# Six early loads and one copy change their places in a hand-ordered attention and feed-forward kernel

## The chip, the cores and the metric

The kernel runs on one core of one Trainium2 chip. The metric is device time in microseconds (us) of one execution. The kernel before was timed three times: median 570.61 us, 570.03 to 570.77. TensorE is written PE, VectorE DVE, ScalarE ACT, GpSimd POOL and SyncE SP; SP issues nearly every transfer between memory and the core.

## The reference, cut to what matters

An attention with a matrix state (4 batches, 8 heads, 768 steps, 40 elements a head) makes x, and a feed-forward part with a rational activation follows:

```python
for t in range(S):
    m_new = np.maximum(f_gate[:, :, t] + m, i_gate[:, :, t])
    f_stab = np.exp(f_gate[:, :, t] + m - m_new)
    i_stab = np.exp(i_gate[:, :, t] - m_new)
    m = m_new
    C = f_stab * C + i_stab * outer(v[t], k[t])      # 40 x 40 a head
    n = f_stab * n + i_stab * k[t]
    y[t] = sigmoid(o_gate[t]) * (C @ q[t]) / np.maximum(np.abs(n @ q[t]), 1.0)
x = y as [3072, 320]
h = x @ w_in                                         # 320 -> 2048
P = a[0] + a[1] * h + a[2] * h**2 + a[3] * h**3
Q = 1.0 + np.abs(b[0]) * np.abs(h) + np.abs(b[1]) * h**2
out = (P / (Q + 1e-06)) @ w_out                      # 2048 -> 320
```

## The kernel before, in words

**Tiling.** The attention is cut into 24 units (`attention(u)`): one batch and 128 steps, all 8 heads. Two units make 256 rows of x, and for each such pair the feed-forward part runs in 8 slabs of 256 hidden columns (`feed_forward`). The weights come from memory as whole 64-bit words, in pieces named i0 to i7, j0, j1 (of w_in) and o0 to o7 (of w_out). `split64` turns a piece into a high and a low float32 part in steps: `raw` (the load, SP), `s0` (two passes on ACT, the first of them the "fill"), `s1` (two on DVE, "sign" and "join"), `o0` (a cast on ACT), `o2` (a subtraction on POOL).

**Gates.** The first 128 steps of the two gates are prepared ahead of all others by `early()`: some 25 short instructions on DVE whose results (tiles `early_kT` and `early_qA`) three transfers store to scratch in memory (scrF, L528, and twice scrA, L532). These three are the first operations named `gate` on SP that depend on another one. Every unit then reads its gates back, spread over the partitions (`lg_u`: tiles fb, L837, and ab, L843, two transfers each). The rest of the gates goes through `gates()` on DVE, interleaved with the first weight pieces.

**First units.** `ogl_u` loads a unit's output gates (tile og, L1077), `ld_u` its keys (kr, L822) and queries (qn, L823), 160 KB each. POOL scales the keys (`kp_u`), PE transposes them (`tk_u`, into kq), ACT copies the result out (`ek_u`, tile kT), then PE transposes the queries (`tq_u`, into the same bank), ACT copies those (`eq_u`, tile qb), and PE multiplies the two (`S_u`, tile ps). DVE multiplies ps with the decay matrix e, which a scan over fb makes (`sc_u`), and PE goes on to y. Until there is real work, PE runs 90 products of the identity with itself (`hot`).

**What sets the order.** Every operation is added to one list with an engine, an estimated cost, a key and its dependencies. `_Plan.order()` simulates the engines and returns one sequence of all operations; the program is written out in it, and each engine works through its own operations strictly in that sequence. So an operation that waits holds up all that stands behind it on its engine. Large tables (NUDGE and others) give the keys; they are the same before and after.

**Transfers of SP.** A transfer waits for the data it reads, for its tile to be free, and for a semaphore: the eight named DMAHW0 to DMAHW7 are handed out in turn, so a transfer is issued only when the one eight places ahead of it has landed.

Of the kernel before, what the change touches and what calls it, by code (L numbers as in the profile page):

```python
# [314 lines left out]
def kernel(tc: tile.TileContext, *args):  # L315


    with ExitStack() as ctx:
        common = _prologue(ctx, tc, args)
        flag = common.pop("flag")()  # L320
        with tc.If(flag > 0) as test:
            _program(tc, True, common, *args)
        with test.Else():
            _program(tc, False, common, *args)
# [51 lines left out]
def _program(  # L376
# [36 lines left out]
    plan = _Plan(START)  # L413
# [684 lines left out]
    def feed_forward(n, i):  # L1098
# [147 lines left out]
        if i == NS - 1:  # L1246
            for t in range(2):
# [2 lines left out]
                add("ev", e, 0.32, lambda t=t, e=e: f_ev(t, e), w=[po[t], o],  # L1250
                    new=[(o, ("ot", BUFS["ot"]))], lag=2.5)


    stg = ctx.enter_context(tc.tile_pool(name="stage", bufs=2))
    ap1 = ctx.enter_context(tc.tile_pool(name="att1", bufs=1))
# [18 lines left out]
        attention(u)  # L1274
    for s in range(NS * (NU // 2)):
        feed_forward(*divmod(s, NS))
    for i in plan.order():
        plan.ops[i][4]()


# [28 lines left out]
```

## Time and profile before

| | |
|---|---|
| median of three runs | 570.61 us (570.03 to 570.77) |
| the profiled execution | 571.71 us |
| its span, first to last instruction | 569.9 us |
| busy: PE, DVE, ACT, POOL | 527.2, 476.2, 430.9, 394.5 us |
| on the chain that ended last | PE 69%, DVE 13%, POOL 5%, ACT 4%, DMA 2% |

The span of the profiled execution leaves out 1.8 us around it, and the execution took 1.1 us longer than the median of the runs. Starts are counted from the span's start. Busy time is the sum over all stages; the first 60 us and the rest have different limits. PE's busy time holds the `hot` products, which nobody waits for.

### The profile page before, as it was taken

Reading aid. Unit: us, or ns where it says so; the run is one execution under the profiler, and the core shown is the slowest. Engines: PE = TensorE matmul, PEld = TensorE weight load, DVE = VectorE, ACT = ScalarE, POOL = GpSimd, SP = SyncE. Lnnn points to the kernel's source line nnn. Section 1 sums busy time; section 2 is a strip of 40 time slices with the busy share of each in tenths; the row PEclk is TensorE's granted clock in tenths of the full one; section 3 lists DMA queues with packets and bytes.
Section 4 is the critical chain, followed back from the end, with each engine's and each line's share of the span. In section 5 each row is a group of like instructions: output and inputs, shape, how many; then the busy total and the mean of one; then the engine's idle time right before and its main releaser. Section 6 shows DMA issues by size and latency. Waiting matters only on the chain.

```text
span 569.9 us, 13096 instructions
## 1 busy us (share of the span) xinstructions
PE 527.2 (93%) x5024; PEld 493.6 (87%) x5024; DVE 476.2 (84%) x782; ACT 430.9 (76%) x757; POOL 394.5 (69%) x353
## 2 busy tenths in 40 slices
PE   4966896899999999999999999999999999999994
PEld 4964686799989999999999898899899999999993
DVE  8999888997888779988888877877987878878685
ACT  2567679776866888777788868888877777777982
POOL 4538469986677697777868684586777686757753
PEclk9877687999999999999999999999999999999998
DMA  5899966432331213332313214232122010000000
GB/s 171 183 258 243 224 170 139 85 69 56 88 66 55 60 45 81 62 72 78 79 35 85 36 50 97 64 66 74 33 62 73 15 36 2 1 26 1 23 1 30
DMA packets 120666, 44.10 MB, mean 77 GB/s; under 512 B 103826, under 2 KB 113106, under 8 KB 120594
## 3 DMA queue, kind: packets, MB, share of 16 engines
q1 hardware_dynamic: 120450, 43.01, 32.3%
q8 instruction: 41, 0.67, 0.5%
q14 instruction: 31, 0.25, 0.2%
q10 hardware_dynamic: 144, 0.16, 0.1%
HBM read 39.03 MB, written 4.13 MB: 76 GB/s over the span
## 4 chain that ended last, share of the span: by engine, by line
PE 69%; DVE 13%; POOL 5%; issue 4%; ACT 4%; DMA 2%; SPq 2%; DVEq 0%; POOLq 0%; ACTq 0%
PE ph L34 27%; PE po L34 25%; PE y L34 7%; PE ps L34 4%; PE kq L34 3%; PE ow L34 2%; DVE w L34 2%; DVE gH L34 2%; POOL p L34 2%; DVE gL L34 1%; ACT ph L34 1%; PE px L34 1%; DVE early_kT L34 1%; POOL w L34 1%; POOL tm L34 1%
## 5 line engine op out<-in xcount | busy, mean ns | idle before, releaser
L34 POOL TENSOR_TENSOR p<-p,w 128x512 f32<-128x512 f32 (+1 forms) x97 | 128.8, 1328 | 84.8 <-DVE w L34 78.1
L34 PE MATMUL ph<-xk,wi 128*128 128x256 f32 x1152 | 174.7, 287 | 0.9 <-DVE gL L34 0.7
L34 POOL TENSOR_TENSOR w<-w,ha 128x512 f32<-128x512 f32 (+1 forms) x97 | 138.5, 1428 | 36.4 <-ACT w L34 32.5
L34 PEld LDWEIGHTS ph<-xk,wi 128*128 128x128 f32 x1152 | 152.8, 189 | 6.0 <-issue 2.1
L34 PE MATMUL po<-wo,gH 128*128 128x320 f32 x768 | 135.8, 315 | 1.8 <-DVE gH L34 1.8
L34 PEld LDWEIGHTS po<-wo,gH 128*128 128x128 f32 x768 | 114.9, 188 | 4.8 <-DVE gH L34 2.6
L34 DVE SCALAR_TENSOR_TENSOR gH<-p,ps,ph 128x512 fp32r<-128x512 f32 (+1 forms) x97 | 71.6, 738 | 33.9 <-PE po L34 15.2
L34 ACT ACTIVATE ha<-ph 128x512 f32<-128x512 f32 (+1 forms) x97 | 57.4, 592 | 42.6 <-PE ph L34 42.3
L34 DVE SCALAR_TENSOR_TENSOR w<-w,gH 128x512 f32<-128x512 f32 (+1 forms) x97 | 84.3, 871 | 5.7 <-POOL p L34 0.5
L34 ACT ACTIVATE w<-ha,ba 128x512 f32<-128x512 f32 (+1 forms) x97 | 78.7, 811 | 4.8 <-POOL p L34 0.4
L34 ACT ACTIVATE ph<-w,cd 128x512 f32<-128x512 f32 (+1 forms) x97 | 66.2, 683 | 20.3 <-DVE p L34 14.4
L34 PE MATMUL po<-wo,gL 128*128 128x320 f32 x384 | 77.1, 318 | 4.3 <-DVE gL L34 4.1
L34 DVE SCALAR_TENSOR_TENSOR gL<-p,ps,ph 128x512 fp32r<-128x512 f32 (+1 forms) x97 | 71.2, 735 | 10.4 <-POOL p L34 8.8
L34 DVE SCALAR_TENSOR_TENSOR p<-p,ps,ph 128x512 f32<-128x512 f32 (+1 forms) x97 | 71.0, 736 | 4.3 <-ACT p L34 3.4
L34 PEld LDWEIGHTS po<-wo,gL 128*128 128x128 f32 x384 | 59.3, 188 | 8.4 <-DVE gL L34 6.6
L34 ACT ACTIVATE p<-ph,ps 128x512 f32<-128x512 f32 (+1 forms) x97 | 65.5, 675 | 0.9 <-DVE gL L34 0.7
L34 ACT ACTIVATE ph<-ph 128x512 f32<-128x512 f32 (+1 forms) x97 | 56.1, 579 | 2.7
L34 PE MATMUL ph<-xk,wj 128*128 128x256 f32 x192 | 54.3, 283 | 0.0
L34 PE MATMUL ph<-xk,wY 128*128 128x256 f32 x192 | 53.9, 281 | 0.0
L34 DVE TENSOR_TENSOR_SCAN e<-fb,eye 128x512 f32<-128x512 f32 x24 | 37.1, 1544 | 0.2
L34 PE MATMUL ps<-qb,kT 104*64 104x128 f32 x384 | 28.9, 297 | 8.2 <-ACT qb L34 5.5
L34 PEld LDWEIGHTS ph<-xk,wY 128*128 128x128 f32 x192 | 36.4, 190 | 0.0
(127 smaller groups left out, 788.7 us busy)
## 6 DMA issues: line engine op xcount, KB each, us to landing
fb<-scrF SPq DMA_DIRECT2D x48, 128.0 KB, 3.1
ab<-scrA SPq DMA_DIRECT2D x48, 128.0 KB, 3.3
rawo<-in_moe_w_out_dram SPq DMA_DIRECT2D x8, 640.0 KB, 5.9
rawi<-in_moe_w_in_dram SPq DMA_DIRECT2D x8, 512.0 KB, 5.6
og<-in_o_gate_dram SPq DMA_DIRECT2D x24, 160.0 KB, 3.4
kr<-in_k_dram SPq DMA_DIRECT2D x24, 160.0 KB, 2.8
qn<-in_q_dram SPq DMA_DIRECT2D x24, 160.0 KB, 3.4
vb<-in_v_dram SPq DMA_DIRECT2D x48, 80.0 KB, 2.8
```

The costliest lines, as they stand in the source:

```text
L34: made = fn(*args, **kwargs)
```

## The change

After the plan is made, and only in the variant that these inputs take (`square`), two groups of operations are taken out of the sequence and put at an earlier place, together with whatever they depend on that still stood behind that place. The first group is `ogl_0`, `ogl_1`, `ld_0` and `ld_1` (six transfers), put ahead of the first store of the early gates. The second is `ek_0`, put ahead of the first operation of piece j1 on ACT. Nothing is added and nothing is removed.

```diff
@@ -1250,6 +1250,15 @@
+    def move(order, names, name, kind):
+
+        at = next(k for k, i in enumerate(order) if plan.ops[i][0] == name and kind(i))
+        moved, todo = set(), {i for i in order[at:] if plan.ops[i][0] in names}
+        while todo:
+            moved |= todo
+            todo = {j for i in todo for j in plan.ops[i][5] if j in order[at:]} - moved
+        order[at:] = [i for i in order[at:] if i in moved] + [i for i in order[at:] if i not in moved]
+
@@ -1274,7 +1283,13 @@
-    for i in plan.order():
+    order = plan.order()
+    if square:
+
+        move(order, ("ogl_0", "ogl_1", "ld_0", "ld_1"), "gate", lambda i: plan.ops[i][2] == "SP" and plan.ops[i][5])
+
+        move(order, ("ek_0",), "s0_j1", lambda i: True)
+    for i in order:
         plan.ops[i][4]()
```

On SP, from the load of the first piece of w_out on, before (rawi here is piece i1, of w_in; the names in brackets are what the row waits for):

```order
L720 DMA rawo_225<-in_moe_w_out_dram 128x2x640 [waits DMAHW3_49]
L528 DMA scrF<-early_kT 64x64 [waits DMAHW4_49,DVE_49]
L532 DMA scrA<-early_qA 32x64 [waits DMAHW5_49,DVE_49]
L532 DMA scrA<-early_qA 32x64 [waits DMAHW6_49]
L720 DMA rawi_253<-in_moe_w_in_dram 128x2x512 [waits DMAHW7_49]
L837 DMA fb_265<-scrF 64x512 [waits DMAHW4_49,DMAHW0_49]
```

And the same place after:

```order
L720 DMA rawo_225<-in_moe_w_out_dram 128x2x640 [waits DMAHW3_49]
L1077 DMA og_244<-in_o_gate_dram 128x8x40 [waits DMAHW4_49]
L1077 DMA og_246<-in_o_gate_dram 128x8x40 [waits DMAHW5_49]
L822 DMA kr_248<-in_k_dram 128x8x40 [waits DMAHW6_49]
L823 DMA qn_61<-in_q_dram 128x8x40 [waits DMAHW7_49,Pool_49]
L822 DMA kr_251<-in_k_dram 128x8x40 [waits DMAHW0_49]
L823 DMA qn_135<-in_q_dram 128x8x40 [waits DMAHW1_49,Pool_49]
L528 DMA scrF<-early_kT 64x64 [waits DMAHW2_49,DVE_49]
L532 DMA scrA<-early_qA 32x64 [waits DMAHW3_49,DVE_49]
L532 DMA scrA<-early_qA 32x64 [waits DMAHW4_49]
L720 DMA rawi_263<-in_moe_w_in_dram 128x2x512 [waits DMAHW5_49]
L837 DMA fb_275<-scrF 64x512 [waits DMAHW6_49,DMAHW2_49]
```

The six loads stood some 10 to 20 places further down and now stand ahead of the three stores, of piece i1 and of all that reads the scratch. Through the turn of the semaphores the store scrF now also waits for piece i2 (eight places ahead), the first scrA for rawo, the second for the first og, and piece i1 for the second og.

On ACT, where piece j1 begins, before (rawj is that piece, kT the copy of unit 0's keys; the row ahead is a pass over piece i0):

```order
L34 ACTIVATE zi_401<-rawi_205 128x512
L34 ACTIVATE rawj_360<-rawj_360 128x512 [waits DMAHW2_49,DMAHW1_49]
L34 COPY kT_413<-kq_396 104x512 [waits PE_49]
L34 CAST wi_421<-zi_401 128x512 [waits DVE_49]
L34 ACTIVATE rawi_377<-rawi_377 128x512 [waits DMAHW3_49]
```

And after:

```order
L34 ACTIVATE zi_401<-rawi_205 128x512
L34 COPY kT_407<-kq_396 104x512 [waits DMAHW2_49,PE_49]
L34 ACTIVATE rawj_360<-rawj_360 128x512 [waits DMAHW2_49,DMAHW1_49]
L34 CAST wi_421<-zi_401 128x512 [waits DVE_49]
L34 ACTIVATE rawi_377<-rawi_377 128x512 [waits DMAHW3_49]
```

The copy and the fill of piece j1 have changed places. The sequences of DVE, POOL and PE are the same before and after, but for buffer numbers.

## Rows read from the trace of the kernel before

**Rows 1.** The page, its head and TensorE's busy time (share of the span).

```profile
span 569.9 us, 13096 instructions
PE 527.2 (93%) x5024; PEld 493.6 (87%) x5024; DVE 476.2 (84%) x782; ACT 430.9 (76%) x757; POOL 394.5 (69%) x353
```

**Rows 2.** Busy us in stretches (PE, PEld, DVE, ACT, POOL), granted clock, DMA share, GB/s.

```profile
10.00:14.00 4.00, 1.51 (x7) 1.40 (x8) 3.57 (x16) 2.14 (x5) 0.00 (x0) 0.73 0.98 361
...
24.00:30.00 6.00, 5.25 (x47) 5.06 (x46) 6.00 (x8) 5.29 (x9) 3.93 (x4) 1.00 1.15 166
...
12.00:45.00 33.00, 25.84 (x183) 24.94 (x183) 31.92 (x55) 19.04 (x34) 13.49 (x13) 0.80 1.01 226
...
200.00:560.00 360.00, 353.77 (x3407) 335.01 (x3404) 298.01 (x477) 287.38 (x498) 255.71 (x222) 1.00 0.20 47
```

**Rows 3.** What VectorE waited for, 12 to 62 us (total, times, longest).

```profile
DVE st L34 <- POOL tm L34: 0.5, 1, 0.5
DVE rawi L34 <- ACT rawi L34: 0.4, 1, 0.4
```

**Rows 4.** The chain that ended last, 0 to 100 us (start, us, what).

```profile
30.43 4.81 DMA rawj<-in_moe_w_in_dram
```

**Rows 5.** Timeline of SyncE's queue (start, us from issue to next, what).

```profile
8.44 0.47 SPq L720 DMA_DIRECT2D rawo<-in_moe_w_out_dram  x1
12.76 0.48 SPq L528 DMA_DIRECT2D scrF<-early_kT  x1
...
14.56 0.58 SPq L720 DMA_DIRECT2D rawi<-in_moe_w_in_dram  x1
...
22.35 0.58 SPq L822 DMA_DIRECT2D kr<-in_k_dram  x1
...
29.45 1.58 SPq L720 DMA_DIRECT2D rawj<-in_moe_w_in_dram  x2
```

**Rows 6.** Transfers, single ones of rows 5 (KB, us from issue to landing).

```profile
rawo<-in_moe_w_out_dram SPq DMA_DIRECT2D x1, 640.0 KB, 7.3
...
scrF<-early_kT SPq DMA_DIRECT2D x1, 16.0 KB, 3.1
...
rawi<-in_moe_w_in_dram SPq DMA_DIRECT2D x1, 512.0 KB, 3.9
```

**Rows 7.** Timeline around piece i1 (start, us, engine, what, idle before).

```profile
17.52 1.14 DVE L34 SCALAR_TENSOR_TENSOR rawo<-rawo 128x640 int32<-128x640 int32 x1
...
18.49 0.68 ACT L34 ACTIVATE rawi<-rawi 128x512 int32<-128x512 uint8 x1 [0.70 <-DMA rawi<-in_moe_w_in_dram]
...
21.38 0.35 DVE L34 TENSOR_SCALAR gate_w<-gate_w 128x384 f32<-128x384 f32 x1
...
21.64 0.69 DVE L34 SCALAR_TENSOR_TENSOR rawi<-rawi 128x512 int32<-128x512 int32 x1
...
22.35 1.65 POOL L34 TENSOR_TENSOR wo<-zo,wo 128x640 fp32r<-128x640 f32 x1 [2.70 <-issue]
...
22.52 2.03 DVE L34 SCALAR_TENSOR_TENSOR zj<-zj,rawj 128x512 int32<-128x512 int32 x1
```

**Rows 8.** Timeline around unit 0's keys and piece j1.

```profile
27.26 1.43 POOL L34 TENSOR_TENSOR wY<-zj,wj 64x512 fp32r<-64x512 f32 x1 [0.72 <-ACT wj L34]
...
28.77 0.92 POOL L34 TENSOR_TENSOR kp<-kr,inat 128x320 f32<-128x320 f32 x1
...
35.32 0.67 ACT L34 ACTIVATE rawj<-rawj 128x512 int32<-128x512 uint8 x1 [4.85 <-DMA rawj<-in_moe_w_in_dram]
```

**Rows 9.** Timeline of TensorE, the products ps and y of two units.

```profile
45.95 1.98 PE L34 MATMUL ps<-qb,kT 104*64 104x128 f32 x16 [2.54 <-ACT qb L34]
...
48.79 1.94 PE L34 MATMUL y<-vb,pm 128*64 128x41 f32 x32
...
67.82 1.09 PE L34 MATMUL ps<-qb,kT 104*64 104x128 f32 x16 [0.63 <-ACT qb L34]
...
69.76 1.13 PE L34 MATMUL y<-vb,pm 128*64 128x41 f32 x32
```

## The prediction

> **What bounds the kernel now.** I read the page first, then the busy time by stretches, then the waits of VectorE, and last the timeline of the stretch that the change touches. The page shows TensorE busy for 93% of a span of 569.9 us [rows 1]. From 200 to 560 us it is busy for 353.8 of 360 us: there the kernel is bound by TensorE, and nothing in the change reaches that stretch except by when it begins. The start is different. From 12 to 45 us VectorE is busy for 31.9 of 33 us [rows 2], and in 12 to 62 us it waits in two places only, 0.5 and 0.4 us [rows 3]. The identity products fill TensorE in that time, so its busy time there says nothing. So the start is bound by VectorE, which works in strict sequence through gates and weight pieces; a time is gained there only where VectorE waits less, and lost wherever it waits more. The chain that ended last names something else, 4.8 us of waiting for piece j1's load [rows 4]. Read together with rows 3, that wait is ScalarE's, and of it only 0.4 us reached VectorE. That is the trap of this profile: the chain follows the last release at each step, not the engine that had no time to spare.
>
> **The second move, the copy ahead of j1's fill.** ScalarE sat idle for 4.85 us until j1 landed, with the finished transpose of unit 0's keys behind it [rows 8]. After the change the copy goes out when the transpose is there. The key's scaling on POOL begins at 28.77, directly after the piece in front of it (27.26 + 1.43 = 28.69), so the transpose is no earlier than before, and the copy comes some 4 to 5 us earlier. Who is glad of that? TensorE's transpose of the queries, and after it nobody: the first real product, ps, stands at 45.95 and waits for ScalarE's qb [rows 9], which in ScalarE's sequence is behind several weight pieces that wait for VectorE. The cast and the fill behind j1 come earlier too, and with them VectorE's wait of 0.4 us goes [rows 3]. What is late next is VectorE itself. I take -0.40 us; the other wait of rows 3, for POOL's tm, stays. The bound of the gain in the direction of the chain is the whole 4.8 us; I take the near end because VectorE, busy for 97% of that stretch, could not use more.
>
> **The first move, six loads ahead of the stores.** The six loads themselves are awaited by nobody at their new place: the keys are first used at 28.77, held up by POOL's own sequence and not by a load [rows 8], and the output gates are used on ScalarE behind the same pieces as before. Their issues, about 0.6 us each [rows 5], fit into the hole in SP's queue between 8.91 and 12.76 us. So the gain of moving them is nothing at the place where they are used; what is left is that the queue behind them gets shorter. Two loads of j1 are issued at 29.45 [rows 5] and land some 5 us later; they may come up to 2 us earlier, which with the copy moved is worth no more than the 0.40 already counted.
>
> The cost is on the transfers that they are put in front of. The hole in SP's issues is not a hole in the DMA engines: from 10 to 14 us their share is 0.98, at 361 GB/s [rows 2]. The early store scrF shows what that means: issued at 12.76, 16 KB only, it lands after 3.1 us, at 15.9; rawo, issued at 8.44, lands at 15.7 [rows 5, 6]. So a transfer lands in line behind those issued ahead of it. After the change the line behind rawo is six loads, three stores, and then piece i1. A load of 160 KB in such short rows goes at the 166 GB/s of the stretch 24 to 30 us, where these loads are all that moves [rows 2]: 164 kB / 166 GB/s = 0.99 us, six of them 5.9 us. The stores take about 0.2 us each (15.9 against 15.7), together 0.6 us. Piece i1 has 524 kB, at 361 GB/s 1.45 us. It lands at 15.7 + 5.9 + 0.6 + 1.45 = 23.65 us; before it was issued at 14.56 and landed 3.9 us later, at 18.5. Its new issue (it has to wait for the second og, 15.7 + 2 x 0.99 = 17.7 us) is in time for that.
>
> Behind it is ScalarE's fill, 0.68 us, and then VectorE's sign pass over i1, which VectorE reached at 21.73, the end of the row in front (21.38 + 0.35) [rows 7]. Now the fill ends at 23.65 + 0.05 + 0.68 = 24.38. VectorE waits 2.65 us, with everything behind it: the next gates, pieces j0 and i1, the decay matrix of unit 0. ScalarE's cast of wo stands behind the same fill, so POOL has nothing to do in that hole either, and the piece wo that in the rows 7 blocks VectorE's zj (2.03 us beside POOL's 1.65, against 0.69 for a pass of that size) comes that much later as well, and blocks again. The readers of the scratch, fb and ab, are issued from about 22.2 us on, some six us later than before, but the scan that reads fb stands behind all passes over i1 in VectorE's sequence, so by then they have landed; and six issues fewer stand between them and j1, so SP is back in step there. The bounds of the 2.65: if i1 were not held in line and needed its old 3.9 us from issue, 17.7 + 3.9 + 0.73 - 21.73 = 0.6 us. If rawo too shares the engines with the six loads, it lands 5.9 us later, at 21.6; with a fill of about 0.7 us VectorE, which passes over rawo at 17.52 [rows 7], is held until about 22.4, 4.9 us. I take 2.65 since scrF's landing in line is a row, and sharing is none.
>
> The Trainium skill has a rule for this in "DMA: Bandwidth & Descriptors", section "Queues, rings and completion order": each DMA engine takes its descriptors in ring order, yet completion is not first-in first-out for the issuing engine, so a later transfer may be done before an earlier one. By the first half the 2.65 us stand; by the second i1 could land ahead of the loads, and the wait would go towards 0.6 us. scrF, 0.2 us behind rawo [rows 5, 6], agrees with the first half, and no row here shows an overtaking.
>
> The sum: +2.65 - 0.40 = +2.25 us. The profiled execution would go from 571.7 (569.9 in the span) to 574.0 us; since it stood 1.1 us above the median of the runs, the forecast against that median is 570.6 + 2.25 = 572.9 us. What VectorE loses reaches the end because TensorE's full stretch waits for the same pieces and units. If a part is taken up by the waits behind 45 us, that is the way to the first rival.
>
> "SBUF — State Buffer", section "Who interferes with whom", in the Trainium skill, says that VectorE and POOL hold a shared pair of ports in turn, whoever begins first blocking the other for the whole instruction. zj's 2.03 us beside POOL's wo agree [rows 7]. By that rule an instruction of VectorE that now begins first escapes once, 1.3 us, and POOL's next piece is late for it, so that the sum stays 2.25 but is blurred by about that much.
>
> **The rivals.**
> First, no stall that counts: piece i1 lands as soon after its issue as before, or the lateness is taken up further on. For it: VectorE is not full after 45 us and waits for POOL [rows 3]. Against it: the DMA share of 0.98. Time: 0.6 - 0.4 = +0.2, 570.8 us.
> Second, the other side: the start gets shorter by TensorE's clock. The products ps and y of unit 0 take 1.98 and 1.94 us, those of a later unit 1.09 and 1.13 [rows 9]: about the ratio of the granted clock's two levels, 1.2 and 2.4 GHz. TensorE had waited 2.54 us in front of that ps. If the earlier transposes shift TensorE's work so that ps and y run at the higher level, and i1 is not late, the gain is 0.89 + 0.81 + 0.40 = 2.1 us: 568.5. It decides only if no gap stands in front of ps; the moved copy rather lengthens that gap, since ps still waits for qb.
> Third, a deeper hole: rawo is late as well, +4.9 - 0.4 = +4.5, 575.1 us. Speaking for it, the engines are full while rawo moves; against it, scrF.
> That the change doesn't do what it says is excluded by the sequences: both groups stand where they should.
>
> **How the numbers follow.** The forecast has 0.58, with an own range of 571.8 to 574.2 (the blur of 1.3 us on either side, and a little more below). The first rival has 0.21, the second 0.14, the third 0.07. The range that leaves out the second alone goes from 569.7 to 575.0 us. A measurement of this kernel can tell a difference of about 0.2%, 1.1 us, from none. Slower by more: nearly all of the forecast and the third, 0.63; within: the first and the forecast's low edge, 0.23; faster: 0.14.
>
> **What would show it.** In the profile after: piece i1's load landing near 23.7 us and the stores near 22; a wait of ScalarE of about 4 to 5 us for rawi, and of VectorE of about 2.6 us behind it near 22 us; the 4.85 us of ScalarE in front of j1 gone; ps near 48 us where it was at 45.95; and from there on the same picture, some 2 us later. The prediction is wrong if i1 lands before 22 us, or if VectorE shows the stall and TensorE's full stretch nevertheless begins no later.

## The result: 573.29 us against 570.54, and the profile after

The changed kernel takes 573.29 us (median of 6 runs, 572.63 to 574.63), the kernel before 570.54 us beside it (568.44 to 570.77). The ratio is 1.0054 with a 95% interval of 1.0037 to 1.007: slower by 2.75 us of medians. The forecast was 572.9 us. The profiled execution of the changed kernel took 573.08 us, its span is 571.2 us; that of before took 571.71. The two profiled executions are thus only 1.4 us apart, half of what the medians are; where the other half is comes at the end of this section.

The waits of VectorE from 12 to 62 us, to be held against [rows 3] (total, times, longest, in us):

```profile
DVE rawi L34 <- ACT rawi L34: 3.8, 1, 3.8
DVE st L34 <- POOL tm L34: 0.5, 1, 0.5
```

There is the stall that was forecast as 2.65 us, and it measures 3.8 us; the wait of 0.4 us that stood for rawi in [rows 3], near 37 us, is gone. The timeline around the stall (start, duration, instruction, idle time before it and its releaser), which answers to [rows 7]:

```profile
17.52 0.81 DVE L34 SCALAR_TENSOR_TENSOR rawo<-rawo 128x640 int32<-128x640 int32 x1
21.26 0.35 DVE L34 TENSOR_SCALAR gate_w<-gate_w 128x384 f32<-128x384 f32 x1
24.70 0.67 ACT L34 ACTIVATE rawi<-rawi 128x512 int32<-128x512 uint8 x1 [6.24 <-DMA rawi<-in_moe_w_in_dram]
25.41 0.69 DVE L34 SCALAR_TENSOR_TENSOR rawi<-rawi 128x512 int32<-128x512 int32 x1 [3.80 <-ACT rawi L34]
26.12 1.65 POOL L34 TENSOR_TENSOR wo<-zo,wo 128x640 fp32r<-128x640 f32 x1 [6.22 <-issue]
26.29 2.04 DVE L34 SCALAR_TENSOR_TENSOR zj<-zj,rawj 128x512 int32<-128x512 int32 x1
```

Read it from the bottom up: VectorE's pass over i1, at 21.64 in [rows 7], stands at 25.41, directly behind ScalarE's fill, which begins 0.02 us after the load of i1 lands at 24.68. POOL's wo and VectorE's zj come as a pair 3.77 us later than before, and zj pays its 2.04 us beside wo again. The pass over rawo is at 17.52 as before: rawo is not what stalls.

Why i1 lands at 24.68 is to be seen in SP's queue, against [rows 5] (start, duration of the issue; x2 is two issues and their sum):

```profile
8.44 0.47 SPq L720 DMA_DIRECT2D rawo<-in_moe_w_out_dram  x1
8.96 3.54 SPq L1077 DMA_DIRECT2D og<-in_o_gate_dram  x2
12.55 3.45 SPq L822 DMA_DIRECT2D kr<-in_k_dram  x1
16.11 0.51 SPq L823 DMA_DIRECT2D qn<-in_q_dram  x1
16.67 0.69 SPq L822 DMA_DIRECT2D kr<-in_k_dram  x1
17.46 0.64 SPq L823 DMA_DIRECT2D qn<-in_q_dram  x1
18.20 0.90 SPq L528 DMA_DIRECT2D scrF<-early_kT  x1
19.19 1.18 SPq L532 DMA_DIRECT2D scrA<-early_qA  x2
20.43 0.58 SPq L720 DMA_DIRECT2D rawi<-in_moe_w_in_dram  x1
```

An issue of such a load cost 0.6 us in [rows 5]. Here the first two took 3.54 us together and the third 3.45 us alone, so that SP, which the forecast had finished with the loads before 12.76 us, stands inside them until 18.1. Neither of the long issues was waiting for its semaphore: the transfers eight places ahead of them had landed at 9.34 and 9.79 us. The hole in its queue was used up and more: scrF goes out at 18.20 instead of 12.76, and i1 at 20.43 instead of 14.56. i1 lands 4.3 us after that, hardly more than its 3.9 us of [rows 6]. So of the 6.2 us by which i1 lands later (24.68 against 18.47), 5.9 us are a later issue.

Full engines are not enough to hold an issue. From 24 to 30 us of the kernel before, the DMA share is 1.15 [rows 2], and loads of the same kind are issued there in 0.6 us each:

```profile
25.26 0.62 SPq L822 DMA_DIRECT2D kr<-in_k_dram  x1
25.97 0.56 SPq L823 DMA_DIRECT2D qn<-in_q_dram  x1
```

The second move did what it says. The chain of waits no longer goes through j1 but through i1 (start, duration; compare [rows 4]), and ScalarE's copy now stands in front of j1's fill, which waits 1.06 us instead of the 4.85 of [rows 8]:

```profile
20.43 4.26 DMA rawi<-in_moe_w_in_dram
24.70 0.68 ACT rawi L34
```

```profile
32.53 0.92 POOL L34 TENSOR_TENSOR kp<-kr,inat 128x320 f32<-128x320 f32 x1
34.63 0.59 ACT L34 COPY kT<-kq 104x512 f32<-104x512 f32 x1 [0.38 <-PE kq L34]
36.29 0.67 ACT L34 ACTIVATE rawj<-rawj 128x512 int32<-128x512 uint8 x1 [1.06 <-DMA rawj<-in_moe_w_in_dram]
49.50 1.97 PE L34 MATMUL ps<-qb,kT 104*64 104x128 f32 x16 [5.77 <-ACT qb L34]
52.35 1.93 PE L34 MATMUL y<-vb,pm 128*64 128x41 f32 x32
```

j1 itself lands at 36.20, about 1 us later than before (35.24), not earlier. The first products ps and y keep their 1.97 and 1.93 us of [rows 9] and stand 3.55 us later.

**How much of the 3.8 us reaches the end.** Taking the same instruction of VectorE in both profiles, the changed kernel is behind by 3.76 us at 31 us, by 3.52 us until 77 us, by 2.05 us from 84 us on, and by 1.37 us from 441 us to the end. So two pieces came back in this pair of profiles. The first lies in the stretch 74 to 86 us (length; busy time and count of PE, weight loads, VectorE, ScalarE, POOL; PE's granted clock; DMA share; GB/s), before and after:

```profile
74.00:86.00 12.00, 11.86 (x129) 10.66 (x128) 10.13 (x20) 8.38 (x17) 8.54 (x8) 0.89 0.65 168
```

```profile
74.00:86.00 12.00, 10.48 (x141) 9.27 (x138) 11.55 (x22) 10.12 (x20) 8.91 (x8) 1.00 0.63 166
```

Before, TensorE worked there at a mean granted clock of 0.89 and VectorE waited 1.1 us for its product ow; after, the clock is 1.00, more products fit into the same time, and that wait is not there. The second piece, 0.7 us at 441 us, lies at one pass of VectorE, which waited for POOL and took 1.51 us before, and took 0.69 us without a wait after:

```profile
441.50 1.51 DVE L34 SCALAR_TENSOR_TENSOR w<-w,gH 128x512 f32<-128x512 f32 x1 [0.46 <-POOL p L34]
```

```profile
443.18 0.69 DVE L34 SCALAR_TENSOR_TENSOR w<-w,gH 128x512 f32<-128x512 f32 x1
```

At neither place stands anything that was moved, and both vary between the profiles: see below for the first; the pass takes 1.51 us in copy_only, two_loads and nine_loads too. The medians, 2.75 us apart, are the better measure of the change; they are 1.0 us short of the stall.

### The profile page after: what moved, and what is told of

Same layout as the page of the kernel before. It is cut to its first block, busy times and chain, and to the rows that moved or that the text cites. A ratio compares the mean times of both kernels' runs of the same rounds, so it can differ in the third digit from the quotient of the medians.

```text
span 571.2 us, 13097 instructions
## 1 busy us (share of the span) xinstructions
PE 523.1 (92%) x5024; PEld 490.4 (86%) x5024; DVE 475.8 (83%) x782; ACT 431.0 (75%) x757; POOL 395.2 (69%) x353
## 4 chain that ended last, share of the span: by engine, by line
PE 69%; DVE 14%; POOL 6%; issue 5%; ACT 3%; DMA 1%; DVEq 0%; SPq 0%; POOLq 0%; ACTq 0%
PE ph L34 27%; PE po L34 26%; PE y L34 7%; PE ps L34 3%; PE kq L34 3%; PE ow L34 2%; DVE w L34 2%; DVE gH L34 2%; POOL p L34 1%; PE px L34 1%; DVE gL L34 1%; POOL w L34 1%; ACT ph L34 1%; DVE rawi L34 1%; DVE st L34 1%
## 5 line engine op out<-in xcount | busy, mean ns | idle before, releaser
L34 PE MATMUL ps<-qb,kT 104*64 104x128 f32 x384 | 27.3, 286 | 10.3 <-ACT qb L34 7.5
```

The costliest lines, as they stand in the source:

```text
L34: made = fn(*args, **kwargs)
```

## The experiments

The theory at this point: i1's lateness is the whole loss, the copy's move is worth nothing or a little, and the lateness comes from transfers that stand in front of i1. Each diff is against the changed kernel; each time is a median with the median of the kernel before on the same chip, and the ratio with its 95% interval; the ratio need not be the quotient of the two medians. The medians of before are 570.97 us for the first four runs and 570.99 us for the last four.

**copy_only: the second move alone.**

```diff
-        move(order, ("ogl_0", "ogl_1", "ld_0", "ld_1"), "gate", lambda i: plan.ops[i][2] == "SP" and plan.ops[i][5])
```

> Only the second move is made: the copy of unit 0's keys stands ahead of piece j1's fill on ScalarE, the six loads stay where they were. Theory (the loss is piece i1's late load, which VectorE waits for near 22 us): no loss, VectorE's 0.4 us wait near 37 us gets shorter, time 0.4 us under the kernel before, 570.1 us; piece i1's fill on ScalarE begins at 18.5 as before. Rival (the loss comes with the copy: TensorE finishes its transposes earlier, stands still longer ahead of ps and works at the lower clock for longer): 1 to 2 us over the kernel before, 571.5 to 572.5 us, with a later start of the full stretch of TensorE and no stall of VectorE near 22 us.

Measured: 571.34 us, ratio 1.0007 (0.9992 to 1.0022): no difference. The copy goes out at 30.28 instead of 35.90, and nobody is the faster for it:

```profile
30.28 0.59 ACT L34 COPY kT<-kq 104x512 f32<-104x512 f32 x1
36.28 0.65 ACT L34 ACTIVATE rawj<-rawj 128x512 int32<-128x512 uint8 x1 [5.42 <-DMA rawj<-in_moe_w_in_dram]
```

ScalarE still waits its five us for j1, now behind the copy instead of in front of it, and VectorE waits 1.2 us for j1's fill, since j1 happens to land at about 36.2 here. The 0.40 us that the forecast took from this move can't be seen. The wait was for the load, not for the copy. (The profiled execution, 573.32 us, is the slowest of the twelve, and VectorE ends 1.6 us behind the profile of before in it; see the last part of this section.)

**loads_only: the first move alone.**

```diff
-        move(order, ("ek_0",), "s0_j1", lambda i: True)
```

> Only the first move is made: the six loads ahead of the three stores, the copy stays behind piece j1's fill. Theory (piece i1 late): VectorE's stall near 22 us is 3.8 us as in the changed kernel, and since j1 lands at 36 us while VectorE comes to its pass over j1 near 39.6 us, the copy's place makes no difference: 573.3 us, within 0.6 us of the changed kernel. Rival (the copy is what costs): 570.5 to 571 us.

Measured: 573.97 us, ratio 1.0042 (1.0023 to 1.0061). i1 lands at 25.64, and VectorE waits 4.8 us for it:

```profile
25.67 0.67 ACT L34 ACTIVATE rawi<-rawi 128x512 int32<-128x512 uint8 x1 [7.49 <-DMA rawi<-in_moe_w_in_dram]
```

In this execution TensorE's granted clock from 74 to 86 us is 0.86, nothing is given back there, and VectorE is behind by 4.7 us at 31 us and still by 4.4 at 277; at the end it is 3.8. The first move alone brings a loss that can't be told from the changed kernel's (the intervals overlap); single executions differ much, from 570.95 to 576.06 us.

**piece_first: both moves, but i1's load is issued in front of the six loads.** This takes away only the lateness of i1; the loads still stand in front of the stores.

```diff
+        move(order, ("raw_i1",), "ogl_0", lambda i: True)
```

> Both moves, and the load of piece i1 moved too, directly ahead of the six loads: i1 in time, the three stores of the early gates still behind the loads. (One load of output gates also comes ahead of fb.) Theory (i1 late): i1 lands near 18 us, ScalarE's fill begins there, VectorE's stall near 22 us is gone altogether, and the time is 0 to 0.5 us under the kernel before, 570.0 to 570.5 us, although the stores still land near 22 to 24 us and fb and ab are read back six us later than before. Rival (the stores are late, so are fb, ab and the decay matrix of unit 0): 2 us or more over the kernel before, 572.5 us and up, with VectorE waiting for fb ahead of the first scan near 32 us.

Measured: 569.9 us, ratio 0.9993 (0.9975 to 1.001). i1 lands at 16.60, its fill runs in time, and VectorE's wait near 22 us is gone:

```profile
17.09 0.66 ACT L34 ACTIVATE rawi<-rawi 128x512 int32<-128x512 uint8 x1
```

```profile
DVE st L34 <- POOL tm L34: 0.5, 1, 0.5
DVE rawj L34 <- ACT rawj L34: 0.2, 1, 0.2
```

SP stalls in the loads as long as in the changed kernel, and the stores go out and land as late as there:

```profile
9.57 3.30 SPq L1077 DMA_DIRECT2D og<-in_o_gate_dram  x2
12.92 3.31 SPq L822 DMA_DIRECT2D kr<-in_k_dram  x1
18.94 0.67 SPq L528 DMA_DIRECT2D scrF<-early_kT  x1
22.08 1.39 SPq L837 DMA_DIRECT2D fb<-scrF  x2
```

So late stores, late readers of the scratch and a stalled SP cost nothing measurable by themselves. Of the orders that compute the same it has the lowest median, 3.4 us below the changed kernel's, and it is no different from the kernel before.

**stores_first: the six loads behind the stores, still in front of i1.**

```diff
-        move(order, (...), "gate", lambda i: plan.ops[i][2] == "SP" and plan.ops[i][5])
+        move(order, (...), "raw_i1", lambda i: True)
```

> Both moves, but the six loads stand behind the three stores and still directly ahead of piece i1: stores in time, i1 late. Theory (i1 late): the stores land near 16 us as before; the loads are issued from 14.6 us on and move 6 us of traffic ahead of i1, which lands near 23 to 25 us; VectorE stalls for 2.5 to 4 us near 22 us; 572.5 to 573.8 us. Rival (the stores late): no loss, 570.0 to 570.8 us.

Measured: 574.61 us, ratio 1.0062 (1.0041 to 1.0082). The stores land at 15.7 to 16.0 as in the kernel before; i1 is issued at 19.20, earlier than in the changed kernel, and lands at 26.30, later:

```profile
12.75 0.48 SPq L528 DMA_DIRECT2D scrF<-early_kT  x1
26.33 0.67 ACT L34 ACTIVATE rawi<-rawi 128x512 int32<-128x512 uint8 x1 [8.80 <-DMA rawi<-in_moe_w_in_dram]
```

VectorE waits 5.3 us, more than the 2.5 to 4 expected. That clears the stores from the other side. It also shows that i1's landing does not always follow its issue. The last of the six loads lands near 22.6; the scratch's first readers, free to go since the stores are early, are issued from 20.02 us, right behind i1, and take 6.5 us while i1 takes 7.1. The two run side by side; that they share the engines and so slow each other is the likely reading, and no run separates them.

**two_loads: only unit 0's keys and queries moved. nine_loads: three more output gates moved.**

```diff
-        move(order, ("ogl_0", "ogl_1", "ld_0", "ld_1"), "gate", ...)
+        move(order, ("ld_0",), "gate", ...)                     # two_loads
+        move(order, ("ogl_0", "ogl_1", "ld_0", "ld_1", "ogl_2", "ogl_3", "ogl_4"), "gate", ...)   # nine_loads
```

> As the changed kernel, but of the six loads only the keys and queries of unit 0 (two loads) stand ahead of the stores. Theory (each load ahead of piece i1 delays it by about 1 us of engine time, and VectorE has some 2 us of room before it comes to i1): i1 lands near 20 us, fill done by 20.8, VectorE's stall near 22 us under 0.3 us, time as the kernel before, 570.3 to 571.0 us. Rival (any load ahead of the stores costs, since SP's queue is held up by it): 571.8 us or more.

> As the changed kernel, with three more loads of output gates (units 2 to 4) moved ahead of the stores: nine loads. Theory (about 1 us a load): i1 lands near 27.5 us, VectorE's stall near 22 us is 6.5 to 7.2 us against 3.8 to 4.8 with six loads, time 2.5 to 3.5 us over the changed kernel, 576 to 577 us. Rival (the delay is one of the queue's turn and not of the traffic, so that it does not grow with the number): as the changed kernel, 573 to 574 us.

Measured: two loads 570.35 us, ratio 1.0008 (0.9986 to 1.0031); nine loads 577.55 us, ratio 1.0124 (1.0096 to 1.0151). ScalarE's fills of i1, in that order:

```profile
21.21 0.69 ACT L34 ACTIVATE rawi<-rawi 128x512 int32<-128x512 uint8 x1 [3.69 <-DMA rawi<-in_moe_w_in_dram]
```

```profile
27.46 0.67 ACT L34 ACTIVATE rawi<-rawi 128x512 int32<-128x512 uint8 x1 [10.32 <-DMA rawi<-in_moe_w_in_dram]
```

Together with [rows 6, 7] and the changed kernel this is a line of four points. With 0, 2, 6 and 9 loads in front, i1 lands at 18.5, 21.2, 24.7 and 27.4 us: 1.4 us for each of the first two loads, 0.9 us for each of the others. Most of that is its issue, which goes out at 14.56, 16.46, 20.43 and 22.62 us; from there it takes 3.9, 4.7, 4.3 and 4.8 us. VectorE's wait is 0, 0.2, 3.8 and 6.6 us, and the ratios are 1, 1.0008, 1.0054 and 1.0124, by which the nine loads cost about 7.1 us (6.6 us by the medians). Their 577.55 us are a little more than the 576 to 577 expected. Two loads fit into the slack between i1's old landing and VectorE's need at about 21 us; by the same step a third would not, but no run has three.

**long_rows: the six loads with the same bytes in 1280-byte rows.** 128 contiguous rows of 1280 bytes are read instead of 1024 rows of 160; the first two units so get other data.

```diff
+            if square and u < 2:
+                flat = [x[b].rearrange("h t d -> (h t d)")[0 : P * H * D].rearrange("(p e) -> p e", p=P) for x in (k, q)]
...
```

> As the changed kernel, but the six moved loads read 160 KB each in 128 rows of 1280 bytes instead of 1024 rows of 160 bytes; so the first two units get other keys, queries and output gates than the reference's. Theory (a load's price is the time its short rows take on the DMA engines, 1 us, and SP's issues are held up by that backlog): at the rate of the weight pieces a load takes 0.45 us, six 2.7 us; SP's issues of the loads take 0.6 us each; i1 lands near 20.7 us; VectorE's stall is under 0.5 us; time 570.2 to 571.0 us. Rival (bytes or the place in the queue count, not the rows): stall as in the changed kernel, 3.8 us or more, 573 to 574 us.

Measured: 570.38 us, ratio 0.9981 (0.9963 to 0.9999). SP's issues, and what became of i1:

```profile
9.06 1.28 SPq L1084 DMA_DIRECT2D og<-in_o_gate_dram  x2
10.38 0.49 SPq L824 DMA_DIRECT2D kr<-in_k_dram  x1
20.81 0.70 ACT L34 ACTIVATE rawi<-rawi 128x512 int32<-128x512 uint8 x1 [3.02 <-DMA rawi<-in_moe_w_in_dram]
```

No issue of a load is held, the loads land 0.4 us apart instead of 0.84, i1 is issued at 16.91 and lands at 20.79, and VectorE doesn't wait. It is the number of short rows, not the bytes, that fills both SP's time and the line. What still makes i1 2.3 us later than before is the turn of the semaphores: the stores scrF and the first scrA go out at 14.03 and 15.75 us, right after the pieces eight places ahead of them have landed (13.97 and 15.69). The run brought something else: VectorE was ahead of the kernel before by 5.1 us at 31 us, and had lost it all by 40 us.

```profile
22.34 7.22 POOL L34 TENSOR_TENSOR wo<-zo,wo 128x640 fp32r<-128x640 f32 x1 [2.71 <-issue]
22.52 0.68 DVE L34 SCALAR_TENSOR_TENSOR zj<-zj,rawj 128x512 int32<-128x512 int32 x1
32.84 0.92 POOL L34 TENSOR_TENSOR kp<-kr,inat 128x320 f32<-128x320 f32 x1
34.95 0.59 ACT L34 COPY kT<-kq 104x512 f32<-104x512 f32 x1 [5.84 <-PE kq L34]
36.14 0.89 DVE L34 SCALAR_TENSOR_TENSOR rawj<-rawj 128x512 int32<-128x512 int32 x1 [2.95 <-ACT rawj L34]
```

At the same starts as in [rows 7] (22.35 and 22.52 there) the outcome is the opposite: VectorE's zj runs free in 0.68 us, and POOL's wo, 1.65 us of work, shows a row of 7.22 us. POOL's scaling of the keys is then 4 us late (32.84 against 28.77), and the copy, which the second move has put in front of j1's fill, holds ScalarE for it, though j1 landed at 32.31. VectorE pays with 2.95 us. By these rows the second move costs VectorE those 2.95 us in such an execution, where in [rows 8] it seemed to save; no run has the long rows without it.

**squares_late: piece_first, with six short instructions of VectorE moved from near 40 us to unit 1's normaliser near 65 us.** If VectorE's own time alone bounded the start, that time would be gained.

```diff
+        late = [i for i in order if plan.ops[i][0] == "ba"]
+        order = [i for i in order if i not in late]
+        at = next(j for j, i in enumerate(order) if plan.ops[i][0] == "rc_1")
+        order[at:at] = late
```

> The order of the run with piece i1 ahead of the six loads, and in addition VectorE's six tiny instructions on the activation's coefficients (1.2 us near 40 us, first used near 78 us) moved back to where VectorE waits, ahead of unit 1's normaliser near 65 us. Theory (the start is bound by VectorE, a microsecond of it is a microsecond of the kernel): VectorE runs 1.2 us ahead of the kernel before from 42 us on, of which 0.3 us is given back near 65; time 0.9 us under that run, 569.0 us. Rival (the chain through the loads and ScalarE bounds the start, not VectorE's own time): no difference, 569.9 us.

Measured: 570.13 us, ratio 1.0 (0.9979 to 1.002): no gain is seen. VectorE is 0.3 us ahead of the kernel before at 47 us, where 1.2 us were expected, and it waits more:

```profile
DVE rawj L34 <- ACT rawj L34: 0.8, 1, 0.8
DVE rawo L34 <- ACT rawo L34: 0.4, 1, 0.4
DVE rawi L34 <- ACT rawi L34: 0.2, 1, 0.2
```

The largest of these waits stands ahead of the place from which the six instructions were taken (40.34 in the kernel before), so it doesn't come from the move:

```profile
36.66 0.69 DVE L34 SCALAR_TENSOR_TENSOR rawj<-rawj 128x512 int32<-128x512 int32 x1 [0.76 <-ACT rawj L34]
```

In this execution j1 landed at 35.90, against 35.19 in piece_first. Behind that place VectorE does win 0.9 us: it goes from 0.63 us behind the kernel before at 39 us to 0.27 ahead at 42. The two smaller waits, at 51.02 and 52.85, stand in copy_only as well (0.4 and 0.2 us), where nothing was taken from VectorE. So the theory is neither shown nor refuted: the 0.9 us expected lie within the interval, which is about 1.1 us wide on either side. What the waits for j1 do show, here, in copy_only and in two_loads (0.8, 1.2 and 0.8 us, j1 landing at 35.9 to 36.2), is that the forecast's sentence "the start is bound by VectorE" holds only nearly: j1 lands so close to the time at which VectorE comes to it that VectorE waits as soon as it lands somewhat later.

**What varies from run to run.** From 74 to 86 us TensorE's granted clock is 0.89 before, 0.86 in loads_only and two_loads, 0.94 in nine_loads, and 1.00 in the other six profiles. The stretch holds the same work only up to VectorE's lag: in nine_loads, the latest, the clock is 1.00 from 76 to 88 us, where that work stands. Where the clock was 1.00 over that work, about 1.5 us come back: VectorE's lag goes from 3.52 to 2.05 us in the changed kernel, from 5.17 to 3.71 in stores_first, from 6.51 to 5.04 in nine_loads, and from -0.01 to -1.48 in piece_first. In loads_only and two_loads nothing comes back (4.53 to 4.50, 0.95 to 0.92). copy_only and long_rows take a course of their own: they gain by 84 us (lags of -0.55 and -1.93) and have lost 2.1 and 2.5 us by 277 us (1.60 and 0.53); from 86 to 104 us their clock is 0.72, against 0.81 in the kernel before. No experiment set this clock on purpose. What brings it about, and whether the change shifts its odds, stays open; if it does, it could account for the 1.0 us between the stall and the medians, which no run shows. Each kernel has one profile, and its medians come from 6 or 12 executions.

## Why the prediction was right, step by step

- **Place: right. Mechanism: right in what waits, not in how i1 comes late.** The loss is VectorE's wait for i1 near 22 us. Each run's time goes with the wait for i1 in its own trace: no such wait in copy_only and piece_first, no loss; 3.8, 4.8, 5.3 and 6.6 us in the changed kernel, loads_only, stores_first and nine_loads, and ratios of 1.0054, 1.0042, 1.0062 and 1.0124 (the intervals of the first three overlap). But the forecast had i1 go out at 17.7 us and wait 5.95 us in the line of the transfer engines; it went out at 20.43 us and took 4.26 us. Most of its lateness is that of its issue.
- **The hole in SP's queue: wrong.** The forecast said that the six issues, about 0.6 us each, "fit into the hole in SP's queue"; the second and third took about 3 and 3.45 us. The duration had come from an issue at 22.35 us [rows 5]. Full engines alone don't hold an issue, as the rows from 25 us above show. What is different near 10 us is that three weight pieces of 512 to 640 KB have been issued and not landed. In stores_first, where the loads go out from 14.55 us on and the last of those pieces lands at 15.45, no issue of a load takes over 0.9 us; in long_rows, with the pieces under way but no short rows, none is held. What exactly holds an issue is not shown. So i1 went out at 20.43, not 17.7, and the three stores came too late to land 0.6 us behind the loads.
- **The terms of i1's landing: three were off, not all in one direction.** Counted as landings one behind the other, rawo landed at 16.38 (15.7 forecast); the six loads took 5.04 us (5.9), their last landing at 21.42; the last store landed 2.03 us after that (0.6); and i1 1.23 us later (1.45): 24.68 instead of 23.65. The stores are the term that was off most; rawo's landing varies between 14.8 and 16.4 us in these profiles. With the fill, and VectorE ready 0.12 us sooner, the wait became 3.80 instead of 2.65 us.
- **Landing in line: seen in piece_first, too strict as a rule.** In piece_first i1 is issued at 9.16, right behind rawo, and lands at 16.60, 1.48 us after it (15.12), where the forecast has 1.45 us for such a piece. In the changed kernel the line can't be told from the late issue: i1's old 3.90 us from its issue at 20.43 give 24.33, close to the 24.68 measured. And stores_first shows i1 and the readers of the scratch side by side for 7.1 and 6.5 us. Of the rule that the forecast weighed (the Trainium skill, "DMA: Bandwidth & Descriptors", section "Queues, rings and completion order": descriptors taken in ring order, completion not first-in first-out), piece_first agrees with the first half, and the second half leaves room for what stores_first shows.
- **The -0.40 us of the copy: not seen.** copy_only is at 1.0007. The wait of 0.4 us depended on j1's landing, which lies between 32.3 and 36.7 us in these profiles; that j1 would come earlier was wrong, it came 1 us later.
- **The size in the end: near by two errors.** 3.80 us of wait in place of 2.65, and no gain from the copy in place of 0.40; of the 3.80 the medians show 2.75, beside the 2.25 of the sum, and where the other 1.0 us went is open. That 573.29 us came so near to 572.9 is in part luck. In the profiled pair only 1.37 us are left at the end, after 1.5 us at 74 to 86 us and 0.7 us at 441 us. The range has a slip: 1.3 us below 572.9 is 571.6, so its lower end of 571.8 leaves a little less below, not more.
- **The rivals.** The first (no stall that counts) had its condition nearly met, i1 landing 4.26 us after its issue against 3.90 before; it fell because the issue was 2.7 us later than the 17.7 us that it too was reckoned from. That no stall means no loss is what two_loads and piece_first show. The second (faster by the clock in ps and y) fell as well: both kept their low speed, though the clock did give something back later. The third (rawo late) fell at the unmoved pass at 17.52.
- **VectorE and POOL.** The forecast cited the Trainium skill, "SBUF — State Buffer", section "Who interferes with whom": whoever begins first blocks the other for the whole instruction. (The Trainium skill says this there of VectorE's modes that use both pairs of ports; of an instruction with two inputs, as zj is, it says that it contends with a reading one of POOL.) zj's 2.04 us beside wo agree. long_rows does not: POOL's row begins 0.18 us earlier there and yet lasts 7.22 us while VectorE runs through eleven instructions unhindered. Starts on POOL are rough in the profile, so who held the ports first can't be read from them; a row of 7.22 us on POOL for 1.65 us of work, beside eleven such instructions, is measured, and that the ports are its cause is not shown.

## What to carry to other kernels

A hole in the queue that issues transfers is not room for more of them: ask whether the transfer engines have a hole at the same place, read the price of an issue from a stretch with the same transfers under way, and look who stands behind in the line with the least slack (here i1 had 2.5 us, worth two loads). Read a long wait on the chain together with the waits of the engine that has no time to spare; the 4.85 us of ScalarE in front of j1 were worth nothing that could be measured. When a pair of profiles disagrees with the medians, follow the lag of the same instruction through both: each step in it has a place, and some of them are not the change's.

## What the hardware showed that was not expected

Issues of transfers with 1024 rows of 160 bytes took 0.5 to 1.2 us on SP in most stretches, also while the DMA share was 1.15, and up to 3.45 us behind three weight pieces that had not landed; with the same bytes in 128 rows of 1280 they took 0.33 to 0.7 us in the same place. The held issue also held all that stood behind it on SP, large transfers too. And two instructions, POOL's wo and VectorE's zj, started at 22.35 and 22.52 us in one execution and at 22.34 and 22.52 in another, came out as 1.65 and 2.03 us in the one and as 7.22 and 0.68 us in the other.
